# Ten or seven plain tiles in the first block, and who makes the low parts of the split ones

## The chip, the cores and the metric

The kernel runs on one core of a Trainium2 chip. The metric is the device time of one execution in microseconds (us); a kernel is run several times, and the median counts. The engines are TensorE (PE in the profile, PEld for its weight loads), VectorE (DVE), ScalarE (ACT), GpSimd (POOL) and SyncE (SP, which issues most DMAs). Each takes its instructions in a fixed order and waits for others through semaphores.

## The reference

Three parts run one after the other, all in float32; batch 4, 8 heads, 768 positions, so 3072 tokens of width 256:

```python
state = decay_full * state + sum(Bx, axis=2)          # a scan over chunks, per head
y     = (C @ B.T * L) @ x + (C @ state) * decay       # -> x, 3072 x 256
xn    = x / sqrt(mean(x * x) + 1e-6) * rms_g
g, v  = xn @ w_gate, xn @ w_val                       # 256 -> 1536 each
x     = (g * sigmoid(g) * v) @ w_out                  # 1536 -> 256
r     = maximum(x @ w_in, 0)                          # 256 -> 2048
out   = (s * r * r + b) @ w_out2                      # 2048 -> 256
```

The weights reach the chip as 64-bit floats and are turned into float32 there.

## The kernel before, in words

**Tiles and blocks.** The tokens come as 32 units of 96; seven blocks of 4 or 5 units (384 or 480 columns) go through the gated layer one after the other, then six groups of 512 columns through the second layer. The weights of the gated layer are cut into twelve tiles (F1 = 12) of 128 hidden features: a tile is 128x768 and holds two slices of w_gate, two of w_val and two of w_out. For a tile and a block, PE makes four hidden products (gate and value, two slices each), ACT takes Silu of the gate, DVE multiplies by the value, and PE makes two output products which add to the PSUM tiles o. The output products of a tile are put off until two more tiles have been emitted (LAG = 2).

**Two ways for a product.** A *split* tile uses the type float32r: a number is held as a high part (hi, a cast on ACT) and a low part (lo, number minus high part, on DVE), and `three` makes one product out of three: high times high, low times high, high times low. This needs the split of the weights (w1h, w1l; `split1`, line 745), of the tokens (xth, xtl) and of the activations (hi, lo in `hidden1`, line 799). A *plain* tile multiplies float32 by float32 (`hidden1_plain`, line 815), which the profile records as two records per product, and needs no split.

**The first block.** Blocks 1 to 6 use split tiles only. In block 0 the tiles 0 to 9 (PLAIN = 10) are plain and 10 and 11 are split. The first five plain tiles (HALVES) run in two halves of 192 columns, since the first units' tokens are ready before the others'. Each weight tile is decoded ahead of its use (`decode1`, line 737): five DVE passes over 768 elements (e, raw, w1f, e, w1f) and two on ACT (e, sg). A plain tile's weights stay in w1f until block 1 comes; there `split1` makes w1h and w1l of them (line 1091). The order of tiles in blocks 1 to 6 is ORDER: the split ones of block 0 first, then the plain ones.

**Token work.** Beside the tiles run the steps that make each unit's tokens: scan (DVE), gram products (PE) and m (DVE), y products (PE), squares (ACT), ss (DVE) and rs, a power of 128x2 elements (POOL), xn (ACT), transposes (PE), xth (ACT) and xtl (DVE). Units 4 to 7 are block 1's and are made while block 0 runs.

**The order.** All instructions are first collected in a plan (class `Plan`). `price` gives each a cost (for a POOL tensor_tensor over more than 128 elements n the cost is 3.1 ns x n + 0.06 us), `forward` and `backward` simulate the engines and due times, and `issue` emits the instructions in the order of the best of three passes. A change of any step may so reorder the others. Early gaps of PE are filled with products of ones. The plan has no cost for what an engine does to another that works at the same time, apart from a higher price of the small rs where `now_free` is off.

**Buffers.** Hidden products go to two PSUM buffers (tag h) in turn. The decoded tiles with m < PLAIN lie in the pool wlo, the others in the pool w2 with four buffers, which first hold first_bc and later x1 and raw tiles. The low parts w1l are in wlo as well.

The line numbers of the profile are those of the helper that emits the plan (L371) for nearly all instructions, so groups are told apart by the names of their tiles.

Of the kernel before, what the change touches and what calls it, by code (L numbers as in the profile page):

```python
# [40 lines left out]
LAG = 2  # L41
F1 = 12
F2 = 16
PLAIN = 10
HALVES = 5
ORDER = [*range(PLAIN, F1), *range(PLAIN)]
N2 = 512
# [338 lines left out]
def scan_glu_relu2(ctx: ExitStack, tc: tile.TileContext, bc, xr, aa, cst, w1, w2, gn, sv, bv, out):  # L386
    nc = Plan(tc.nc)
# [35 lines left out]
    w1h = {m: wts.tile([P, 6, P], F32R, tag="w1h", name="w1h") for m in ORDER}  # L423
    w1f, w1l, w2f, w2h = {}, {}, {}, {}
    w2_sum = const.tile([P, 2, P], F32, name="w2_sum")

    def f32(t):
        return t.bitcast(F32)
# [294 lines left out]
    def flat(t):  # L723
        return t.rearrange("p a b -> p (a b)")
# [12 lines left out]
    def decode1(m):  # L737
        if m not in raw1:
            load1(m)
        raw = raw1.pop(m)  # L740
        pool, tag = (wlo, "wlo") if m < PLAIN else (w2_p, "w2")
        w1f[m] = pool.tile([P, 6, P], F32, tag=tag, name="w1f")
        decode(raw, flat(w1f[m]), 6 * P, nc.vector)

    def split1(m):
        w1l[m] = wlo.tile([P, 6, P], F32R, tag="wlo", name="w1l")
        split(flat(w1f.pop(m)), flat(w1h[m]), flat(w1l[m]), nc.vector)


    def decode2(m):  # L750
# [17 lines left out]
    def split(src, hi, lo, rest=nc.vector):  # L768
        nc.scalar.copy(out=hi, in_=src)
        rest.tensor_tensor(out=lo, in0=src, in1=f32(hi), op=ALU.subtract)  # L770
# [44 lines left out]
    def hidden1_plain(j, m, half):  # L815
        n = NB[j] // 2
        cols = slice(0, NB[j]) if half is None else slice(half * n, (half + 1) * n)
        if half is None:
            ps = [ps_h.tile([P, 512], F32, tag="h", name="h")[:, :NB[j]] for v in range(2)]
        else:  # L820
            both = ps_h.tile([P, 512], F32, tag="h", name="h")
            ps = [both[:, v * n:(v + 1) * n] for v in range(2)]
        for v in range(2):
            for k in range(2):
                nc.pace = True
                nc.tensor.matmul(out=ps[v], lhsT=w1f[m][:, 2 * k + v, :],
                                 rhs=rows0[:, k, cols], start=k == 0, stop=k == 1)
                nc.pace = False
        s = hl_p.tile([P, cols.stop - cols.start], F32, tag="hi", name="h32")
        nc.scalar.activation(out=s, in_=ps[0], func=AF.Silu)  # L830
        nc.vector.tensor_tensor(out=s, in0=ps[1], in1=s, op=ALU.mult)

        def out():
            o = [t[:, :NB[j]] for t in o_t[j, 1]]
            for t in range(2):
                nc.pace = True
                nc.tensor.matmul(out=o[t][:, cols], lhsT=w1f[m][:, 4 + t, :], rhs=s,
                                 start=m == 0 and half == 0, stop=False)
                nc.pace = False
        pending.append(out)  # L840
# [151 lines left out]
    def drain(n):  # L992
        while len(pending) > n:
            pending.popleft()()
# [65 lines left out]
    for i in range(F1 + behind):  # L1060
        if i < F1:
            decode1(i)
            if i < HALVES:
                rows0 = xt_h[0]
                hidden1_plain(0, i, 0)
                drain(LAG)
            if i >= PLAIN:
                split1(i)
        tokens_to(count[1] + (count[3] - count[1]) * (i + 1) // behind if i < behind else
                  count[3] + (count[7] - count[3]) * (i + 1 - behind) // F1)  # L1070
        if i - behind == PLAIN:
            xt_h[0] = res_p.tile([P, 2, NB[0]], F32R, tag="res", name="xth0")
            xt_l[0] = [w2f_p.tile([P, NB[0]], F32R, tag="w2f", name="xtl0") for k in range(2)]
            for k in range(2):
                split(rows0[:, k], xt_h[0][:, k], xt_l[0][k])
        if i >= behind:
            if i - behind < PLAIN:
                hidden1_plain(0, i - behind, 1 if i - behind < HALVES else None)
            else:
                hidden1(0, i - behind)  # L1080
            drain(LAG)
# [7 lines left out]
    for i, (layer, j, m) in enumerate(plan):  # L1089
        at = i - start[layer, j]  # L1090
        if (layer, j) == (1, 1) and m < PLAIN:
            split1(m)
        if layer == 1 and 2 <= j < NBLK - 1 and at % 3 == 0:
            nc.floor = nc.latest
            decode2((j - 2) * 4 + at // 3)
            nc.floor = None
        late = at if layer == 1 and j == NBLK - 1 else F1 + m // 2 if (layer, j) == (2, 0) and m % 2 == 0 else None
        if late == 0:
            split_rows(0)
            bias_products()  # L1100
        for q in range(F2 // 2):
            if late == (max(2 * q, 1) if q < 7 else F1 + 2):
                combine(q)
        if layer == 2:
            if m == 0 and (g := j + 1) * N2 < 2 * NPAIR * SEQ:
                split_rows(g)
            if m % 2 == 0:
                seven(j, m // 2)
                drain(LAG)
            continue  # L1110
        hidden1(j, m)
        drain(LAG)
        for (i0, n0), (i1, n1) in zip(marks, marks[1:]):
            if i0 <= i < i1:
                tokens_to(n0 + -(-(n1 - n0) * (i + 1 - i0) // (i1 - i0)))
# [74 lines left out]
```

## Time and profile before

| | |
|---|---|
| median of 3 runs | 628.17 us (627.4 to 629.59) |
| span of the profiled execution | 626.8 us |
| PE busy | 617.4 us, 98% |
| DVE busy | 484.0 us, 77% |
| ACT busy | 447.5 us, 71% |
| POOL busy | 53.6 us, 9% |
| share of PE in the chain that ended last | 95% |
| granted TensorE clock, mean | 0.999 |

The span reaches from the first to the last instruction of one profiled execution; a run's time holds some 1.3 us more than that. Busy shares are means over stages of different kind, so the stages are read one by one below: up to about 30 us the weights and first tokens arrive, block 0 ends at about 74.5 us, block 1 follows, and so on. A row of a timeline gives start, duration, engine, line, operation, output and inputs, and count; neighbouring instructions of one kind are merged, and the duration is then that from the first start to the last end.

### The profile page before, as it was taken

How to read it: one execution, taken by the hardware profiler on the slowest of the kernel's cores; microseconds unless marked ns; L12 is line 12 of the kernel's file. 1: busy time of each engine (PE TensorE's matmuls, PEld its weight loads, DVE VectorE, ACT ScalarE, POOL GpSimd, SP SyncE). 2: the span in 40 equal slices, each digit the busy share in tenths (PEclk: the TensorE clock that was granted, in tenths of full speed). 3: DMA queues.
4: the chain of work that ended last, by engine and by line, in shares of the span. 5: the costliest groups of instructions: out<-in, count | busy, mean ns of one | idle time of the engine just before them, and what ended most of it. 6: DMA issues, size and time to landing. Idle time of an engine off the chain costs nothing.

```text
span 626.8 us, 12902 instructions
## 1 busy us (share of the span) xinstructions
PE 617.4 (98%) x4937; PEld 546.9 (87%) x4937; DVE 484.0 (77%) x972; ACT 447.5 (71%) x941; POOL 53.6 (9%) x88
## 2 busy tenths in 40 slices
PE   9999999999999999999999999999999999999996
PEld 8786899999988888888888889999999999999986
DVE  7999965778756765766865568798897897987975
ACT  5797553766645545664664579898898999988985
POOL 3001100010100001102232220000000000000000
PEclk9999999999999999999999999999999999999999
DMA  6966413424404423400100000001010010010101
GB/s 219 245 216 186 130 29 67 89 70 102 112 34 89 104 81 86 105 20 2 27 2 1 0 2 0 2 5 31 1 34 1 2 35 0 9 28 1 33 1 36
DMA packets 33695, 35.01 MB, mean 56 GB/s; under 512 B 14048, under 2 KB 30048, under 8 KB 33632
## 3 DMA queue, kind: packets, MB, share of 16 engines
q1 hardware_dynamic: 32688, 33.71, 20.9%
q8 instruction: 39, 0.64, 0.4%
q10 hardware_dynamic: 944, 0.46, 0.3%
q14 instruction: 24, 0.20, 0.1%
HBM read 30.90 MB, written 3.25 MB: 54 GB/s over the span
## 4 chain that ended last, share of the span: by engine, by line
PE 95%; ACT 2%; DMA 1%; DVE 1%; issue 0%; DVEq 0%; ACTq 0%
PE h L371 54%; PE o L371 22%; PE acc L371 13%; PE y L371 5%; DMA raw<-in_w 1%; PE o L364 1%; ACT sg L371 0%; ACT xh L371 0%; DVE res L371 0%; ACT xn L371 0%; ACT e L371 0%; PE ab L371 0%; DVE m L371 0%; ACT xth L371 0%; DVE a_sb L371 0%
## 5 line engine op out<-in xcount | busy, mean ns | idle before, releaser
L371 ACT ACTIVATE s<-h 128x512 f32<-128x512 f32 (+2 forms) x170 | 97.3, 572 | 44.0 <-PE h L371 40.7
L371 ACT CAST hi<-s 128x256 fp32r<-128x256 f32 (+2 forms) x170 | 80.1, 474 | 64.4 <-DVE s L371 62.3
L371 PE MATMUL h<-x1h,w2h 128*128 128x512 f32 x384 | 119.2, 391 | 0.0
L371 DVE TENSOR_TENSOR lo<-s,hi 128x256 fp32r<-128x256 f32 (+2 forms) x170 | 86.9, 512 | 30.8 <-ACT hi L371 28.3
L371 PE MATMUL h<-xth,w1h 128*128 128x480 f32 (+1 forms) x296 | 109.9, 371 | 0.5 <-DVE s L371 0.5
L371 PE MATMUL h<-xth,w1l 128*128 128x480 f32 (+1 forms) x296 | 109.0, 368 | 0.0
L371 PE MATMUL h<-xtl,w1h 128*128 128x480 f32 (+1 forms) x296 | 107.8, 367 | 0.0
L371 PE MATMUL acc<-hi,w2c 128*128 128x256 f32 x448 | 81.7, 281 | 0.0
L371 PEld LDWEIGHTS h<-x1h,w2h 128*128 128x128 f32 x384 | 69.2, 188 | 12.3
L371 DVE TENSOR_TENSOR s<-h,s 128x480 f32<-128x480 f32 (+1 forms) x74 | 45.8, 619 | 41.7 <-PE h L371 36.1
L371 PE MATMUL h<-x1l,w2h 128*128 128x512 f32 x192 | 75.0, 390 | 0.0
L371 PEld LDWEIGHTS acc<-hi,w2c 128*128 128x128 f32 x448 | 71.0, 189 | 2.3
L371 DVE TENSOR_TENSOR added<-s 128x256 f32<-128x256 f32 x144 | 56.6, 421 | 13.4 <-ACT s L371 12.4
L371 PE MATMUL acc<-lo,w2c 128*128 128x256 f32 x224 | 63.2, 282 | 0.0
L371 PEld LDWEIGHTS h<-xth,w1h 128*128 128x128 f32 x296 | 55.5, 188 | 7.7 <-DVE s L371 1.0
L371 ACT ACTIVATE s<-s 128x512 f32<-128x512 f32 x96 | 60.2, 633 | 1.9
L371 PEld LDWEIGHTS h<-xth,w1l 128*128 128x128 f32 x296 | 55.6, 188 | 6.1 <-issue 0.2
L371 PEld LDWEIGHTS h<-xtl,w1h 128*128 128x128 f32 x296 | 55.6, 188 | 5.6 <-issue 0.2
L371 PE MATMUL o<-hi,w1l 128*128 128x480 f32 (+1 forms) x148 | 54.2, 367 | 0.0
L371 PE MATMUL o<-hi,w1h 128*128 128x480 f32 (+1 forms) x148 | 54.1, 366 | 0.0
L371 PE MATMUL o<-lo,w1h 128*128 128x480 f32 (+1 forms) x148 | 53.9, 365 | 0.0
L371 DVE TENSOR_TENSOR lo<-added,hi 128x768 fp32r<-128x768 f32 x48 | 45.9, 957 | 0.5 <-ACT hi L371 0.5
(98 smaller groups left out, 1071.0 us busy)
## 6 DMA issues: line engine op xcount, KB each, us to landing
raw<-in_w SPq DMA_DIRECT2D x12, 768.0 KB, 5.4
raw<-in_w SPq DMA_DIRECT2D x16, 512.0 KB, 3.7
a_sb<-a_scr SPq DMA_DIRECT2D x28, 196.0 KB, 3.9
xh<-in_xr SPq DMA_DIRECT2D x60, 48.0 KB, 1.9
raw_bc<-in_bc SPq DMA_DIRECT2D x56, 32.0 KB, 3.8
raw_bc<-in_bc SPq DMA_DIRECT2D x112, 16.0 KB, 1.7
out_t<-res SPq DMA_DIRECT2D x13, 96.0 KB, 1.9
out_t<-res SPq DMA_DIRECT2D x5, 144.0 KB, 1.9
```

Source lines behind the costliest of these rows:

```text
L364: self.nc.tensor.matmul(out=idle, lhsT=ones, rhs=ones, start=not fills, stop=True, skip_group_check=True)
L371: getattr(engine, op["fn"])(*op["args"], **op["kw"])
```

## The change

Two lines. PLAIN goes from 10 to 7, so tiles 7, 8 and 9 run as split tiles in block 0 and ORDER becomes 7 to 11, then 0 to 6. And `split1` takes GpSimd for the low part of the tiles from PLAIN on (7 to 11, in block 0), DVE still for the others (0 to 6, in block 1).

```diff
-PLAIN = 10
+PLAIN = 7
 HALVES = 5
 ORDER = [*range(PLAIN, F1), *range(PLAIN)]
...
     def split1(m):
         w1l[m] = wlo.tile([P, 6, P], F32R, tag="wlo", name="w1l")
-        split(flat(w1f.pop(m)), flat(w1h[m]), flat(w1l[m]), nc.vector)
+        split(flat(w1f.pop(m)), flat(w1h[m]), flat(w1l[m]), nc.vector if m < PLAIN else nc.gpsimd)
```

The function that it calls is unchanged; `rest` is the engine of the low part:

```python
def split(src, hi, lo, rest=nc.vector):
    nc.scalar.copy(out=hi, in_=src)
    rest.tensor_tensor(out=lo, in0=src, in1=f32(hi), op=ALU.subtract)
```

## Rows read from the trace of the kernel before

**Rows 1.** The table of stretches: busy time (x instructions) of each engine, clock, DMA.
```profile
core 0: us, PE busy (x) PEld busy (x) DVE busy (x) ACT busy (x) POOL busy (x), PEclk, DMA share, GB/s
30.00:62.00 32.00, 31.43 (x257) 24.14 (x263) 31.84 (x61) 27.48 (x55) 2.69 (x1) 1.00 0.66 205
62.00:87.00 25.00, 25.00 (x244) 21.76 (x227) 24.63 (x44) 12.29 (x32) 2.19 (x1) 1.00 0.35 97
87.00:112.00 25.00, 25.00 (x314) 23.79 (x313) 11.73 (x25) 11.97 (x34) 0.69 (x1) 1.00 0.34 64
```
**Rows 2.** The chain that ended last, 30 to 90 us: start, us, what.
```profile
43.76 2.58 PE h L371 x8
...
54.88 1.29 PE o L371 x4
...
80.05 2.12 PE h L371 x12
82.17 1.05 PE o L371 x6
```
**Rows 3.** The timeline of DVE at the end of block 0.
```profile
61.45 0.95 DVE L371 TENSOR_TENSOR w1f<-w1f,e 128x768 f32<-128x768 f32 x1
...
62.78 1.41 DVE L371 TENSOR_TENSOR m<-y,a_sb 128x384 f32<-128x384 f32 x4
64.11 0.95 DVE L371 TENSOR_TENSOR w1l<-w1f,w1h 128x768 fp32r<-128x768 f32 x1
...
66.77 0.95 DVE L371 TENSOR_TENSOR w1l<-w1f,w1h 128x768 fp32r<-128x768 f32 x1
...
67.71 0.95 DVE L371 TENSOR_TENSOR w1f<-w1f,e 128x768 f32<-128x768 f32 x1
68.58 0.95 DVE L371 TENSOR_TENSOR w1l<-w1f,w1h 128x768 fp32r<-128x768 f32 x1
...
69.92 0.95 DVE L371 TENSOR_TENSOR w1l<-w1f,w1h 128x768 fp32r<-128x768 f32 x1
...
71.66 0.54 DVE L371 TENSOR_TENSOR lo<-s,hi 128x384 fp32r<-128x384 f32 x1
```
**Rows 4.** The timeline of ACT: the casts of tiles 10 and 11.
```profile
62.43 0.84 ACT L371 CAST w1h<-w1f 128x768 fp32r<-128x768 f32 x1
...
68.70 0.83 ACT L371 CAST w1h<-w1f 128x768 fp32r<-128x768 f32 x1
```
**Rows 5.** Groups by line and shape, 0 to 70 us: busy, mean ns | idle before.
```profile
L371 ACT CAST w1h<-w1f 128x768 fp32r<-128x768 f32 x12 | 9.8, 856 | 0.1
```
**Rows 6.** The timeline of POOL; in brackets the idle time before and its releaser.
```profile
67.89 2.19 POOL L371 TENSOR_TENSOR rs<-ss,fixed 128x2 f32<-128x2 f32 x1 [11.69 <-DVE ss L371]
...
157.57 0.74 POOL L371 TENSOR_TENSOR w_sum<-w_sum,w2f 128x256 f32<-128x256 f32 x1 [10.66 <-DVE w2f L371]
...
295.97 0.47 POOL L371 TENSOR_TENSOR sums<-w2f 128x128 f32<-128x128 f32 x1
...
303.08 1.50 POOL L371 TENSOR_TENSOR sums<-w2f 128x256 f32<-128x256 f32 x1
...
315.88 0.79 POOL L371 TENSOR_TENSOR w_sum<-w_sum,w2f 128x256 f32<-128x256 f32 x1
```
**Rows 7.** The timeline of DVE beside the POOL operation of 303.08.
```profile
303.96 0.77 DVE L371 TENSOR_TENSOR w2c<-w2f,w2c 128x128 fp32r<-128x128 f32 x1
```
**Rows 8.** The tile w2c, 314 to 318 us: duration ns min/median/max, first and last start.
```profile
L371 DVE TENSOR_TENSOR w2c<-w2f,w2c x6: 280/286/823, 314.2 to 316.7; 128x128 fp32r<-128x128 f32 x6
```
**Rows 9.** Groups of DVE by shape, 46 to 69 us: those that read PSUM.
```profile
L371 DVE TENSOR_TENSOR h<-h,h 128x384 f32<-128x384 f32 x5 | 2.8, 553 | 0.0
...
L371 DVE TENSOR_TENSOR m<-y,a_sb 128x384 f32<-128x384 f32 x4 | 2.0, 550 | 0.0
...
L371 DVE SCALAR_TENSOR_TENSOR xtl<-y,sb,xth 128x96 fp32r<-128x96 f32 x4 | 1.0, 312 | 0.0
L371 DVE TENSOR_TENSOR m<-y,a_sb 128x128 f32<-128x128 f32 x4 | 1.0, 282 | 0.0
```
**Rows 10.** The timeline of PE where block 1 begins.
```profile
74.53 0.34 PE L371 MATMUL h<-xth,w1h 128*128 128x384 f32 x1
```

## The prediction

> **What bounds the kernel now.** I read the table of stretches first. From 30 us on TensorE (PE) is busy almost without a gap, and up to 87 us VectorE (DVE) is too: 31.84 of 32 us, then 24.63 of 25. Only after 87 us does DVE fall to 11.73 of 25 [rows 1]. So the first block, which ends near 74.5 us, has two engines that are full at once. After it PE alone sets the time, and whatever the first block loses or gains goes unchanged to the end. Then I read the chain of waits for PE's price of a tile, the timelines of DVE and ScalarE (ACT) for the end of the block, and the rows where GpSimd (POOL) works beside DVE. The profiled span is 626.8 us and the median of the runs 628.17, so 1.3 us lie around the span; I work out the difference on the span and add it to the median.
>
> **PE.** The eight records of a plain tile's four hidden products take 2.58 us in the chain, its four output records 1.29, together 3.87 us. A split tile's twelve hidden products take 2.12 us, its six output products 1.05, together 3.17 us [rows 2]. Three tiles change sides: 3 x 0.70 = 2.1 us less PE work, all ahead of block 1. That is the most the change can give.
>
> **DVE, what leaves.** The subtraction that makes a low part is a 128x768 DVE pass: 0.95 us recorded, 0.87 from start to start. Tile 10's decode ends at 61.45 + 0.95 = 62.40, ACT casts it at 62.43, so its low part is the pass at 64.11. Tile 11's decode ends at 67.71 + 0.95 = 68.66, its cast starts at 68.70, so its low part is that at 69.92. The passes at 66.77 and 68.58 belong to tiles that block 1 needs [rows 3, 4]. The change gives the low parts of tiles 10 and 11 to POOL, and the one at 66.77 is no longer urgent, since block 1 starts with five tiles already split. Ahead of the end of tile 11's decode DVE so loses 2 x 0.87 = 1.74 us (64.11 and 66.77).
>
> **DVE, what comes.** A split tile also needs the low part of its own activations, a 128x384 subtraction of 0.54 us (71.66), about 0.46 in a dense row [rows 3]. Tiles 7, 8 and 9 add 3 x 0.46 = 1.4 us. ACT adds three casts of about the same size. Between 62 and 87 us it is busy 12.29 of 25 us [rows 1], and all twelve weight casts already lie before 70 us [rows 5], so ACT's part costs nothing; without that cover it would be half a microsecond a cast.
>
> **DVE, what GpSimd does to it.** The trace has no 128x768 POOL subtraction. Its nearest rows are 128x128 in 0.47 us and 128x256 in 0.74: 2.1 ns an element more, so 0.74 + 512 x 2.1 ns = 1.8 us for 768 elements, an estimate from these two [rows 6]. That is twice DVE's time, but POOL is nearly idle. What matters is DVE beside it. At 303.96 a w2c subtraction takes 0.77 us, while a POOL addition of 128x256 runs to 303.08 + 1.50 = 304.58 [rows 6, 7]; six such subtractions near 315 us take 0.28 us at the least, 0.29 in the middle and 0.82 at the worst, and that one stands beside the POOL addition of 315.88 [rows 6, 8]. The two lose 0.49 and 0.54 us against 0.28, or 1.9 to 2.1 ns for each of the 256 elements: DVE stands still for nearly as long as POOL runs. For 768 elements this makes 1.6 us a tile, more than the 0.87 that DVE is spared.
>
> [...]
>
> The other end is zero. A two-element rs operation on POOL at 67.89 takes 2.19 us, while the DVE pass inside it (68.58) keeps its 0.95 us: there POOL did the waiting [rows 3, 6]. And DVE passes that read PSUM need not be stopped: m, h and xtl from y take 2.0 + 1.0 + 2.8 + 1.0 = 6.8 of the 23 us from 46 to 69 us [rows 9]. What of a POOL operation falls beside them would cost DVE nothing. So the loss of a tile lies between 0 and 1.6 us. Three tenths off give 1.1; and as the m passes at 62.78 stand where tile 10's low part becomes ready [rows 3], I take 1.0. Four tiles (7 to 10) fall ahead of the end of tile 11's decode: 4.0 us, with ends 0 and 6.4.
>
> **The end of block 0.** PE takes its instructions in order. Tile 11's second product needs the low part, and behind it stand the rest of tile 11 and all of block 1, which begins at 74.53 today [rows 10]. In the changed kernel:
> - tile 11's decode ends later by 4.0 + 1.4 - 1.74 = 3.7 us;
> - from the cast's end (68.70 + 0.83 = 69.53 [rows 4]) to the end of the DVE low part (69.92 + 0.95 = 70.87) it is 1.34 us; POOL takes 1.8 and perhaps half a microsecond until a DVE pass lets it in, 2.3: 1.0 us more;
> - the six output products of tile 10, 1.05 us, which stand ahead of block 1 today, can fill PE's wait: 1.05 us back;
> - the order of instructions is planned, and tile 11's decode may go ahead of token work such as the m passes at 62.78. But block 1 waits for that work as well, and both are in one full engine. I give this 1.0 us, with bounds 0 and 2.
>
> Sum: 3.7 + 1.0 - 1.05 - 1.0 = 2.6 us later for block 1. The 2.1 us that PE saves become idle PE time.
>
> **Cost at nothing.** POOL's own queue: rs of the units of block 1 now stands among five operations of about 2 us each, and ACT's scaling, PE's transposes and the xth tiles wait for rs; where rs lands right behind a low part it is up to 2 us late, which the upper end holds. Block 1: DVE has seven low parts left after 74.5 us instead of eight, but PE is busy all the time there [rows 1], so nothing is gained. DMAs: none is moved, and the weights load in the order 0 to 11 as before. Buffers: the decoded tiles 7 to 9 move to another pool, where tile 11 takes the buffer of tile 7; that low part is done some 15 us before. Below nothing: the planner's new order of later instructions could win a few tenths, but PE has no gap there to win.
>
> **Rivals.**
> - *The full gain.* POOL waits, as rs did, and DVE isn't stopped. With no loss the sum is 2.6 - 4.0 = -1.4 us, and with the planner's slack at its bound of 2 us PE's own saving is reached: 628.2 - 2.1 = 626.1 us. For it: the rs row. Against it: the w2c rows, subtractions on both engines as here. It decides below about 0.1 us lost a tile.
> - *A wash.* At 0.4 us a tile the sum is 2.6 - 4.0 + 1.6 = 0.2 us: 628.4. It holds from 0.2 to 0.8 us a tile, 627.6 to 630.0. For it: the PSUM passes, and that the low parts of tiles 7 and 8 come while decoding is still ahead of PE. Against it: most of what DVE has to do reads SBUF twice.
> - *All of it lost.* Each of the four tiles costs 1.6 us and the planner's microsecond goes to a late rs: 6.4 + 1.4 - 1.74 + 1.0 - 1.05 = 6.0 us: 634.2.
> - *Another order only.* The split tiles run so late that they lie among block 1's, DVE's loss is hidden there and PE's saving shows in part: 627 us. Against it: two hidden PSUM buffers hand the tiles over in turn.
>
> **How the numbers follow.** Chances: the forecast 0.47, all of it lost 0.08, the wash 0.31, the full gain 0.11, another order 0.03. The predicted time is 628.2 + 2.6 = 630.8 us, and the forecast's own range 629.6 to 632.5. A difference of 0.3%, 1.9 us, is about what a measurement of this kernel can tell from no change: below 626.3 is faster, above 630.1 slower. Slower: 0.42 of the forecast and all of it lost, 0.50. Faster: the full gain and a little of the last case, 0.13. The rest, 0.37, is the same. The 8-in-10 range runs from just under the full gain, 626.0, to 633.5, short of all of it lost.
>
> **What would show it.** In the changed profile: five POOL subtractions w1l of 1.8 us or more; DVE passes with two SBUF inputs stretched beside them, from 0.95 to 2 us or more; PE waiting for a POOL w1l at tile 11 and perhaps at tiles 9 and 10; block 1's first product at 76 to 78 us against 74.53. The step on DVE is wrong if its passes keep their durations beside POOL; the sum is wrong if block 1 starts before 74 us; and the first block's seven plain tiles must show 2.1 us less PE work, or the change does not do what it says.

## The result and the profile after

The changed kernel takes 634.92 us (median of 4 runs, 634.26 to 636.18) against 628.25 for the kernel before in the same session (4 runs): the ratio is 1.0102, 95% interval 1.0085 to 1.0119, so it is slower by 6.7 us. The forecast was 630.8 us, 2.6 more than before, with a range that ended at 633.5. The profiled execution is the slowest of the four (636.18, span 634.4), so its rows sum to a little more than the median shows. Its time holds 1.8 us more than its span, not 1.3; differences between runs don't feel that.

First the timeline of PE, where block 2 begins. Block 1's first product is a poor marker here, since different output products are still pending when it starts; at block 2 they are all done. The first fence is the kernel before, the second the changed one (start us, us, engine, line, operation, tiles). The row at 71.29 is the second product of tile 11 in the kernel before, the one that needs its low part; it is used further down.

```profile
71.29 0.33 PE L371 MATMUL h<-xth,w1l 128*128 128x384 f32 x1
...
119.56 0.34 PE L371 MATMUL h<-xth,w1h 128*128 128x384 f32 x1
```
```profile
126.40 0.34 PE L371 MATMUL h<-xth,w1h 128*128 128x384 f32 x1
```

Block 2 is 6.84 us late. Nearly all of the loss is there, and nothing after it gives any back: from here to the last instruction the profiled executions differ by another 0.8 us (spans of 634.4 and 626.8).

The table of stretches, which answers to [rows 1], with one more stretch:

```profile
30.00:62.00 32.00, 28.04 (x227) 22.71 (x225) 31.81 (x56) 25.37 (x53) 10.03 (x4) 0.99 0.64 202
62.00:87.00 25.00, 23.44 (x201) 21.81 (x202) 24.13 (x38) 13.23 (x32) 5.63 (x4) 0.88 0.34 99
...
62.00:68.00 6.00, 6.00 (x47) 5.34 (x48) 5.84 (x10) 2.70 (x5) 2.27 (x2) 0.50 0.11 30
```

DVE is as full as before (31.81 of 32 us) and now PE isn't: it is busy for 28.04 us where it was 31.43. In 62 to 68 us its granted clock is 0.50. Next the timelines of POOL, DVE, ACT and PE around the end of block 0, which answer to [rows 3], [rows 4], [rows 6] and [rows 10]:

```profile
52.05 5.08 POOL L371 TENSOR_TENSOR w1l<-w1f,w1h 128x768 fp32r<-128x768 f32 x2
60.62 1.82 POOL L371 TENSOR_TENSOR w1l<-w1f,w1h 128x768 fp32r<-128x768 f32 x1 [3.49 <-ACT w1h L371]
65.06 1.83 POOL L371 TENSOR_TENSOR w1l<-w1f,w1h 128x768 fp32r<-128x768 f32 x1 [2.62 <-ACT w1h L371]
...
73.27 2.10 POOL L371 TENSOR_TENSOR w1l<-w1f,w1h 128x768 fp32r<-128x768 f32 x1 [1.02 <-ACT w1h L371]
...
52.98 2.46 DVE L371 SCALAR_TENSOR_TENSOR w1f<-raw 128x768 f32<-128x768 uint32 x1
55.36 2.19 DVE L371 TENSOR_SCALAR e<-raw 128x768 uint16<-128x768 uint16 x1
...
61.51 1.76 DVE L371 TENSOR_TENSOR_SCAN a_sb<-a_sb,delta 128x392 f32<-128x392 f32 x1
...
64.92 1.39 DVE L371 TENSOR_TENSOR m<-y,a_sb 128x384 f32<-128x384 f32 x4
66.23 1.08 DVE L371 TENSOR_SCALAR e<-raw 128x768 uint16<-128x768 uint16 x1
...
68.88 0.95 DVE L371 SCALAR_TENSOR_TENSOR w1f<-raw 128x768 f32<-128x768 uint32 x1
...
70.21 0.55 DVE L371 TENSOR_TENSOR lo<-s,hi 128x384 fp32r<-128x384 f32 x1
...
70.75 0.95 DVE L371 TENSOR_TENSOR w1f<-w1f,e 128x768 f32<-128x768 f32 x1
...
72.77 3.44 DVE L371 TENSOR_TENSOR_SCAN a_sb<-a_sb,delta 128x392 f32<-128x392 f32 x2 [0.33 <-DMA a_sb<-a_scr]
76.12 0.53 DVE L371 TENSOR_TENSOR s<-h,s 128x384 f32<-128x384 f32 x1
...
77.91 0.55 DVE L371 TENSOR_TENSOR lo<-s,hi 128x384 fp32r<-128x384 f32 x1
...
72.37 0.83 ACT L371 CAST w1h<-w1f 128x768 fp32r<-128x768 f32 x1
...
54.67 0.44 PE L371 MATMUL h<-xth,w1l 128*128 128x384 f32 x1 [1.09 <-POOL w1l L371]
...
59.87 0.44 PE L371 MATMUL h<-xth,w1h 128*128 128x384 f32 x1 [2.10 <-ACT s L371]
...
76.70 0.45 PE L371 MATMUL h<-xth,w1h 128*128 128x384 f32 x1 [1.52 <-DVE s L371]
...
78.14 0.34 PE L371 MATMUL h<-xth,w1l 128*128 128x384 f32 x1
```

Read each POOL row against the DVE rows inside it. The pass w1f<-raw that takes 0.95 us alone (68.88) takes 2.46 at 52.98, the pass e that takes 0.55 alone takes 2.19 at 55.36: 1.51 and 1.64 us lost to the first two subtractions. The third costs a scan 0.79 (1.76 against 0.97), the fourth a pass e 0.53, the fifth the second of the two scans at 72.77 1.60 (the pair takes 3.44, and 1.84 in the run nolock below). That is 6.07 us in all, 4.47 of it ahead of the end of tile 11's decode. The four m passes at 64.92, which read PSUM, keep their duration beside the fourth subtraction (1.39 us, and 1.41 at 62.78 in the kernel before); only the pass behind them is stopped.

The chain of waits of the changed kernel (start, us, what) says what these stops are worth:

```profile
53.00 2.43 DVE w1f L371
55.43 2.13 DVE e L371
...
57.58 0.94 ACT e L371
58.52 0.92 ACT xth L371 x4
59.44 0.39 ACT s L371
...
68.15 4.52 DMA a_sb<-a_scr
...
72.77 1.60 DVE a_sb L371 x2
74.37 1.76 issue
76.12 0.54 DVE s L371
```

Two stopped DVE passes delay e on ACT, which stands ahead of the Silu that PE wants: this is PE's wait of 2.10 us at 59.87. Later the two scans of units 8 and 9 wait for their DMA until 72.77; the fifth stop stands in the chain as 1.76 us of "issue", time in which the profile shows nothing that DVE waited for. Behind it comes s of tile 10 (76.12), for which PE waits. POOL's own result, the low part of tile 11, was ready at 75.37.

### The profile page after: what moved, and what is told of

It reads as the page before. It is cut to its first block, busy times and chain, and to the rows that moved or that the text cites. A ratio compares the mean times of both kernels' runs of the same rounds, so it can differ in the third digit from the quotient of the medians.

```text
span 634.4 us, 12937 instructions
## 1 busy us (share of the span) xinstructions
PE 620.3 (98%) x4943; PEld 551.6 (87%) x4943; DVE 486.8 (77%) x970; ACT 448.4 (71%) x944; POOL 64.3 (10%) x93
## 4 chain that ended last, share of the span: by engine, by line
PE 87%; DVE 5%; ACT 4%; DMA 2%; issue 2%; DVEq 0%; SPq 0%; ACTq 0%
PE h L371 48%; PE o L371 19%; PE acc L371 13%; PE y L371 5%; DMA a_sb<-a_scr 2%; PE o L364 1%; ACT sg L371 1%; DVE w1f L371 1%; DVE s L371 1%; DVE e L371 1%; PE ab L371 1%; ACT e L371 1%; DVE a_sb L371 1%; ACT xth L371 1%; DVE m L371 0%
## 5 line engine op out<-in xcount | busy, mean ns | idle before, releaser
L371 PE MATMUL h<-xth,w1h 128*128 128x480 f32 (+1 forms) x308 | 114.3, 372 | 5.0 <-ACT s L371 2.7
L371 PE MATMUL h<-xth,w1l 128*128 128x480 f32 (+1 forms) x308 | 113.8, 370 | 1.1 <-POOL w1l L371 1.1
L371 PE MATMUL h<-xtl,w1h 128*128 128x480 f32 (+1 forms) x308 | 112.6, 369 | 0.0
L371 DVE TENSOR_TENSOR s<-h,s 128x480 f32<-128x480 f32 (+1 forms) x77 | 47.4, 615 | 42.3 <-PE h L371 36.3
L371 PEld LDWEIGHTS h<-xth,w1h 128*128 128x128 f32 x308 | 58.3, 189 | 13.5 <-ACT s L371 4.0
L371 PEld LDWEIGHTS h<-xth,w1l 128*128 128x128 f32 x308 | 58.3, 189 | 7.8 <-POOL w1l L371 1.7
L371 PEld LDWEIGHTS h<-xtl,w1h 128*128 128x128 f32 x308 | 58.4, 190 | 5.6 <-issue 0.2
L371 PE MATMUL o<-hi,w1h 128*128 128x480 f32 (+1 forms) x154 | 56.5, 367 | 0.0
L371 PE MATMUL o<-hi,w1l 128*128 128x480 f32 (+1 forms) x154 | 56.5, 367 | 0.0
L371 PE MATMUL o<-lo,w1h 128*128 128x480 f32 (+1 forms) x154 | 55.8, 365 | 0.0
```

Source lines behind the costliest of these rows:

```text
L371: getattr(engine, op["fn"])(*op["args"], **op["kw"])
```

## The experiments

Three theories were open. POOL's subtractions stop DVE, and the stops carry the loss. Or three more split tiles cost time by themselves, whoever makes the low parts. Or PE's clock, which fell between 62 and 68 us, carries it. The runs take these one at a time. All times are medians of runs beside the kernel before on the same chip (628.4 to 628.5 us).

**idlepool: the stop alone.** The kernel before, and POOL does five subtractions of 128x768 that nobody reads and nobody waits for:

```diff
+            w = op["kw"].get("out")
+            if op["eng"] == "vector" and op["fn"] == "tensor_tensor" and w.name.startswith("w1f"):
+                self.made += 1
+                if self.made > F1 - 5:
+                    self.nc.gpsimd.tensor_tensor(out=self.spare, in0=w, in1=w, op=ALU.subtract)
```

> The kernel before, every instruction of DVE, ACT, PE and SP in its order, and five GpSimd subtractions 128x768 (w1f minus itself, into a tile that nobody reads), each ready when one of the tiles 7 to 11 is decoded. Nobody waits for their result. Theory A: DVE stops for about 1.2 us beside each; since DVE is full this comes through but for its slack of some 2 us: 631 to 634 us. Rival B (only the wait for the low part matters): 627.5 to 629 us.

631.89 us, ratio 1.0056 (1.0041 to 1.0071): 3.4 us slower, inside the first theory's range. The first of the five, on POOL and beside it on DVE, and an ACT row at the end of the block, in the timelines:

```profile
44.68 2.18 POOL L377 TENSOR_TENSOR spare<-w1f 128x768 bf16<-128x768 f32 x1 [16.77 <-DVE w1f L372]
...
45.95 1.73 DVE L372 SCALAR_TENSOR_TENSOR w1f<-raw 128x768 f32<-128x768 uint32 x1
...
73.62 0.84 ACT L372 ACTIVATE xn<-y,rs 128x256 f32<-128x256 f32 x2 [2.09 <-POOL rs L372]
```

The order of every other engine is that of the kernel before, and nobody waits for these results, yet four DVE passes are 3.5 us longer in sum (0.78 for the one shown, 1.73 against 0.95; then 1.09, 0.80 and 0.81). The fourth subtraction, at 63.89, stands beside m passes that read PSUM (four in 1.41 us at 64.13) and stops nothing. From the first stop to the end of tile 11's decode DVE loses 2.4 us for 2.67 us of stops: tile 7's last decode pass starts at 43.64 us where it was 44.66 before, tile 11's decode ends at 70.02 where it was 68.66. So there a microsecond of stopped DVE is nearly a microsecond of the block. The whole 3.4 us can't be put on the stops alone, though: rs stands behind the fifth subtraction in POOL's queue, ACT waits 2.09 us for it, and DVE then 0.98 us for the hi behind that.

**nolock: the change without the reading.** POOL writes the low parts (one column copied, then two fills with zeros: 1.77 us for the third tile, from 58.94 on, where a lone subtraction takes 1.82) but doesn't read the tiles; the low parts of the five tiles are zero. The order is that of the changed kernel.

```diff
+                engine.tensor_copy(out=lo[:, 0:1], in_=hi[:, 0:1])
+                for _ in range(2):
+                    engine.memset(lo.bitcast(F32), 0.0)
```

> The changed kernel in the same order on every engine, but GpSimd only writes: each of its five 128x768 subtractions is a copy of one column of w1h (which keeps the wait for the cast) and two memsets of w1l; the low parts are zero, so that part of the weights is left out. Theory A (GpSimd's reading stops the DVE passes that read SBUF twice; the changed profile has them 6.1 us longer in all): the passes keep 0.95 and 0.55 us, block 1 starts 5 to 6 us earlier than in the changed kernel, time 627 to 630 us. Rival B (GpSimd's time from cast to low part, and its queue, make PE wait): GpSimd still takes about 1.5 us a tile, so little changes: 632 to 635 us. Rival C (three more split tiles are simply too much for the first block, whoever makes the low parts): 634 to 635 us.

631.99 us, ratio 1.0053 (1.0036 to 1.0069): 2.9 us less than the changed kernel, still 3.5 us more than the kernel before. That is 2 us above the first theory's range and at the lower edge of that of rival B, whose wait shows only at tile 7 (1.04 us, for POOL's w1l at 54.81). POOL, DVE and PE in the timelines of this run, and two stretches of its table:

```profile
53.22 1.53 POOL L375 MEMSET w1l<- 128x768 f32 x2
...
53.16 0.96 DVE L377 SCALAR_TENSOR_TENSOR w1f<-raw 128x768 f32<-128x768 uint32 x1
54.03 1.13 DVE L377 TENSOR_SCALAR e<-raw 128x768 uint16<-128x768 uint16 x1
...
66.95 0.94 DVE L377 TENSOR_TENSOR w1f<-w1f,e 128x768 f32<-128x768 f32 x1
...
70.38 1.84 DVE L377 TENSOR_TENSOR_SCAN a_sb<-a_sb,delta 128x392 f32<-128x392 f32 x2 [2.02 <-DMA a_sb<-a_scr]
...
72.72 0.44 PE L377 MATMUL h<-xth,w1h 128*128 128x384 f32 x1 [1.83 <-DVE s L377]
```
```profile
68.00:73.00 5.00, 3.17 (x18) 2.84 (x17) 2.98 (x5) 2.82 (x7) 2.10 (x4) 1.00 0.64 130
73.00:77.00 4.00, 4.00 (x17) 3.99 (x16) 4.00 (x9) 1.42 (x6) 0.00 (x0) 0.57 0.92 359
```

The stops are gone but for 0.58 us (54.03), and tile 11's decode ends at 67.89, 3.81 us before the changed kernel's 71.70 (70.75 + 0.95). That is the 4.47 - 0.58 = 3.89 us of stops, nearly one for one. At that point nolock is 0.8 us ahead of the kernel before, and yet it ends 3.5 us behind it: DVE stands 2.02 us before the scans, PE 1.83 us for the s behind them, and then PE runs at a granted 0.57.

**double: twice the stops.** Each of POOL's five subtractions is issued twice.

```diff
-            getattr(engine, op["fn"])(*op["args"], **op["kw"])
+            for _ in range(1 + (op["eng"] == "gpsimd" and "out" in op["kw"] and op["kw"]["out"].name.startswith("w1l"))):
+                getattr(engine, op["fn"])(*op["args"], **op["kw"])
```

> The changed kernel with each of the five GpSimd subtractions done twice (the same result), every order unchanged. Theory A: DVE stops for up to 1.6 us more beside each, and PE waits 1.8 us more for each low part: 639 to 643 us, with the DVE passes stretched by 10 to 13 us in all against 6.1. Rival C: the low parts are only a little late: 635 to 637 us.

642.26 us, ratio 1.0215 (1.0198 to 1.0232), inside the first theory's range: 7.3 us more than the changed kernel for five more subtractions, 1.5 each. The timelines of POOL and DVE:

```profile
52.24 13.83 POOL L372 TENSOR_TENSOR w1l<-w1f,w1h 128x768 fp32r<-128x768 f32 x6
...
53.16 2.46 DVE L372 SCALAR_TENSOR_TENSOR w1f<-raw 128x768 f32<-128x768 uint32 x1
55.55 2.15 DVE L372 TENSOR_SCALAR e<-raw 128x768 uint16<-128x768 uint16 x1
```

Here the two engines take turns, one instruction each: six DVE passes in a row, from 53.16 on, are 1.5 to 1.65 us longer, one beside each of the six subtractions, and these take 2.3 us each (13.83 in all), where a lone one takes 1.82. In sum DVE's passes are 14.0 us longer (10 to 13 were expected, 6.07 in the changed kernel), and PE also waits 3.6 us for a low part, so the 7.3 us aren't stops alone. The first theory holds, but for a part of the loss only: idlepool and nolock put the subtractions at about 3 us of the 6.7.

**vec7, vec8, vec9: fewer plain tiles, DVE makes all low parts.** `split1` is that of the kernel before; only PLAIN differs.

```diff
-PLAIN = 10
+PLAIN = 7        # 8 and 9 in the other two
```

> One part alone: seven plain tiles, all low parts on DVE. Theory A: DVE gets 1.4 us for activations and 1.7 us of low parts more ahead of tile 11 than in the kernel before, no stalls: 629 to 631.5 us, clearly below the changed kernel's 634.9. Rival C: 634 to 635.5 us, the same as the changed kernel.

> Eight plain tiles, all low parts on DVE. At 1.2 us a tile: 630.5 to 631.2 us. With slack for one tile only: 629 to 630 us.

> Nine plain tiles, all low parts on DVE. If every tile turned from plain to split costs DVE about 1.2 us in a full first block (three cost 3.7 us): 629.4 to 630 us. If DVE has slack for one (1.7 us of low parts that block 1 needs stand early in the kernel before) and TensorE's 0.7 us come through: 627.5 to 628.2 us.

vec7 632.19 (1.0053, 1.0037 to 1.0069), vec8 630.35 (1.0027, 1.0018 to 1.0037), vec9 628.08 (1.0006, 0.9988 to 1.0023). The 3.7 us of vec7 are above what was expected of it; vec8 lies between its two ranges; vec9 falls in the second of its ranges, that in which DVE has slack for one tile. So the second theory has something in it too: each split tile in the place of a plain one saves PE time on paper, and none makes the kernel faster; one makes no difference, two cost 1.9 us with the granted clock at 1.00 to 87 us, three 3.7 us without any work on POOL. Of these 3.7 most are the clock's, as vec7_awake shows below.

**pool10: only the engine changed.** PLAIN stays 10; POOL makes the low parts of tiles 10 and 11 alone.

```diff
-        split(flat(w1f.pop(m)), flat(w1h[m]), flat(w1l[m]), nc.vector)
+        split(flat(w1f.pop(m)), flat(w1h[m]), flat(w1l[m]), nc.vector if m < PLAIN else nc.gpsimd)
```

> The other part alone: ten plain tiles as before, the low parts of tiles 10 and 11 on GpSimd. Theory A: two GpSimd subtractions stop DVE for 1.2 us each against 1.74 us taken off it, and tile 11's low part comes 1 us later: 628.5 to 630.5 us. Rival C: DVE is relieved, nothing else changes: 627 to 628.3 us.

631.31 us, ratio 1.0047 (1.0034 to 1.0060): 2.9 us for two subtractions, above the expectation. DVE in its timeline:

```profile
62.04 2.10 DVE L371 TENSOR_SCALAR raw<-raw 128x768 int32<-128x768 int32 x1
...
68.06 4.29 DVE L371 TENSOR_TENSOR w1l<-w1f,w1h 128x768 fp32r<-128x768 f32 x3
```

Both stops are whole (1.55 us at 62.04; 1.6 in the row of three, which take 2.7 alone), 3.15 together, while DVE was spared two low parts, 1.74 us. Tile 11's decode ends 1.0 us earlier than in the kernel before (67.66 against 68.66): the loss comes behind it, where the second stop stands ahead of s of tile 10 and PE waits 1.61 us for that s (at 72.94). The two halves of the change, 3.7 (vec7) and 2.9, add to 6.6 of the 6.7 us, but that is chance: 2.7 of vec7's 3.7 are a fall of the clock (next runs), which costs the changed kernel nothing that can be measured.

**vec7_awake, awake, awake2: the clock.** Products of ones that nobody reads keep PE busy where it waited: 44 of them in vec7, ahead of tile 10's first product; 92 in the changed kernel at tiles 7 and 8 (awake); the same and 38 ahead of tile 11's second half (awake2).

```diff
+            for _ in range(self.extra.get(i, 0)):
+                self.nc.tensor.matmul(out=idle, lhsT=ones, rhs=ones, start=False, stop=True, skip_group_check=True)
...
+                nc.extra[len(nc.ops)] = {(7, 1): 40, (8, 0): 40, (8, 1): 12, (11, 1): 38}.get((m, v), 0)
```

> Seven plain tiles with all low parts on DVE, and 44 products of ones put on TensorE ahead of tile 10's first product, where it stalled for 2.5 us in that kernel before it ran at a granted clock of 0.5 from 64.9 to 71.6 us. Theory D (here the clock lies on the path, since DVE then waited 1.4 and 0.9 us for products): the clock stays 1.0 and 1.5 to 2.5 us come back: 629.7 to 630.7 us against 632.2. Rival (DVE alone sets the time, as where the same was tried with GpSimd): 631.7 to 632.7 us.

> The changed kernel with 92 products of ones put on TensorE where it stalled (40 and 12 ahead of tile 8's two halves, 40 ahead of the second half of tile 7), the other engines' order unchanged. Theory D (the granted clock of 0.5 from 61.7 to 68.2 us lies on the path): clock stays 1.0 and 2 to 3 us come back: 632 to 633 us. Theory A (DVE is the bound there, TensorE waits anyway): the clock stays 1.0 and the time stays at 634 to 635.5 us.

> The changed kernel with TensorE kept busy by products of ones that nobody reads: the 92 of the run awake at tiles 7 and 8, and 38 more ahead of tile 11's second half, where awake's granted clock fell to 0.50 (77 to 80 us) once PE had waited 2.1 us for the DVE pass that makes s of tile 10. Nothing else differs, in order or work. If the clock lies on the path that delays the output half of tile 11 and with it block 1: 632.5 to 634 us, with the granted clock at 1.0 up to 85 us and block 2's first product ahead of the 126.4 us that both the changed kernel and awake show. Rival, the DVE queue alone sets that end and PE would have waited for it at either clock: 634 to 635.5 us, block 2's first product at 126 us or later, clock at 1.0 all the same.

vec7_awake 629.53 (1.0012, 1.0001 to 1.0023), just under the range of the theory that the clock counts; awake 635.39 (1.0108, 1.0093 to 1.0123) and awake2 634.76 (1.0100, 1.0085 to 1.0116), both in the range in which it doesn't. The tables of stretches of vec7, vec7_awake, awake and awake2:

```profile
60.00:65.00 5.00, 2.26 (x11) 1.56 (x10) 5.00 (x10) 2.37 (x4) 0.00 (x0) 0.99 0.18 53
65.00:71.00 6.00, 6.00 (x77) 5.67 (x77) 4.62 (x9) 2.88 (x9) 0.69 (x1) 0.50 0.60 113
```
```profile
60.00:65.00 5.00, 4.78 (x79) 4.34 (x80) 5.00 (x11) 2.91 (x4) 0.00 (x0) 1.00 0.14 39
65.00:71.00 6.00, 6.00 (x81) 5.67 (x74) 6.00 (x12) 5.21 (x15) 0.69 (x1) 1.00 0.59 114
```
```profile
77.00:80.00 3.00, 3.00 (x11) 3.00 (x11) 3.00 (x8) 0.74 (x4) 0.00 (x0) 0.50 0.52 202
```
```profile
62.00:68.00 6.00, 6.00 (x127) 5.30 (x127) 6.00 (x10) 3.82 (x6) 2.15 (x2) 1.00 0.12 33
77.00:80.00 3.00, 2.96 (x18) 2.61 (x17) 3.00 (x8) 1.52 (x5) 0.00 (x0) 1.00 0.79 309
```

In vec7 the clock counts. PE had been busy for 2.26 of 5 us, waiting for a cast, and then ran at 0.50; DVE was busy only 4.62 of the next 6 us, since it waited for PE. With the fills both go, and 2.7 us with them; 1.0 us over the kernel before is left. In the changed kernel the clock counts for nothing that can be measured. awake didn't settle that, since its clock fell later instead (77 to 80 us). In awake2 it is at 1.00 in every stretch from 50 to 87 us, PE still waits for s of tile 10 (38 fills and 0.42 us), block 2 begins at 126.06 (126.40 in the changed kernel), and the time is that of the changed kernel. There DVE is last, and a faster PE waits longer.

**late, nolock_late: the scans.** The scans of units 8 and 9 are held back until s of tile 11 has been made, in the changed kernel and in nolock.

```diff
+        after = start[self.release] + 1e-6
+        start = [max(t, after) if i in self.held else t for i, t in enumerate(start)]
...
+            if units[0] == 8:
+                nc.held.add(len(nc.ops))
...
+        if (j, m) == (0, F1 - 1):
+            nc.release = len(nc.ops)
```

> The changed kernel with one thing moved: the two scans of units 8 and 9 (block 2's), which stood on DVE ahead of the activation product s of tile 10 and waited there for their DMA (started at 72.77, done at 76.2 us), come behind the s of tile 11. All other instructions keep their order. Theory E (the place of these scans is a cause of its own): PE's wait of 1.5 us for s goes, 632.5 to 633.7 us against 634.9. Rival (the fifth GpSimd subtraction, done at 75.4 us, ends last anyway, or stops another pass): 634.2 to 635.2 us.

> Both undone: GpSimd only writes (low parts zero, so that part of the weights is left out) and the two scans come late. Theories A and E add up: 2 to 3 us under the 632.0 us of the kernel in which GpSimd only writes, since DVE waited 2.0 us for the DMA there: 629 to 630.2 us, near the kernel before. Rival C (seven plain tiles are too much for DVE): 631 to 632.5 us, no better than with the scans early.

late 634.09 (1.0115, 1.0078 to 1.0151; its six runs spread from 633.69 to 640.28), nolock_late 630.54 (1.0036, 1.0019 to 1.0052). Each lies between its two ranges, late just under the rival's. DVE in the timeline of late:

```profile
72.90 0.56 DVE L374 TENSOR_TENSOR s<-h,s 128x384 f32<-128x384 f32 x1 [0.78 <-PE h L374]
73.38 1.49 DVE L374 TENSOR_TENSOR lo<-s,hi 128x384 fp32r<-128x384 f32 x1
```

With the scans out of the way s of tile 10 starts 3.2 us earlier (72.90 for 76.12), but the fifth subtraction then stops the low part behind it (1.49 for 0.55). The difference to the changed kernel, 0.8 us, can't be told from none. Without stops the same edit gains 1.45 us; since the granted clock then stays at 1.00, where nolock's fell to 0.57, scans and clock can't be told apart in that. The edit has a price of its own, too: in block 1 PE waits 0.76 us (late, at 82.90) and 0.75 us (nolock_late, at 78.88) for an s that now stands behind the scans. Between these two runs, alike in order and both without a fall of the clock, lies the cleanest price of the stops: 634.09 - 630.54 = 3.55 us. nolock_late still stands 2.1 us above the kernel before. PE idles 1.9 of 12 us between 50 and 62 us in it, for POOL's w1l and for s on ACT, nearly what the three tiles save it. How the 2.1 divide further wasn't tried, and what they consist of is not shown.

## Why the prediction was wrong

**PE: right.** The records of full-width plain hidden products in block 0 go from 40 to 16, three tiles' worth. PE's saving did become idle time, as the text had it: 4.0 us idle in 30 to 62 us, 0.6 before. The saving itself was read from the number of records, not measured as 2.1 us.

**What GpSimd does to DVE: right, at the right size.** A lone subtraction takes 1.82 us, as estimated. Four stops ahead of the end of tile 11's decode cost 4.47 us, where 4.0 were taken (1.1 a tile for 1.0). PSUM passes were spared, as supposed (the m passes at 64.92). The two-input pass at 52.98 is stopped for 1.51 us beside a subtraction; in nolock the two-input pass at 53.16 keeps 0.96 us beside a fill. The prediction read 1.6 us a tile from the w2c rows; where a stop isn't covered by other passes it measures 1.51 to 1.64.

**The end of tile 11's decode: right in the sum, by luck in two terms.** Predicted 3.7 later, less 1.0 for the planner: 2.7. Measured 71.70 against 68.66, 3.04 later. Put the measured stops in the place of the 4.0 and the sum is 4.47 + 1.4 - 1.74 - 1.0 = 3.1. nolock tests the same sum without stops: 0.58 + 1.4 - 1.74 - 1.0 = -0.8 us, and its decode ends 0.77 us early. But the planner's 1.0 us isn't what it was said to be. Just as many passes of token work stand ahead of the decode's end as before (8 scans, 16 m passes, 4 xtl from y). What stands behind it instead is work of the split tiles: two low parts of activations came ahead of it and not three (the second is the one at 70.21), and one product with the value fewer, together about 0.9 us.

**The rest of "The end of block 0": wrong.** This is the step that failed. From 2.7 late at the decode the prediction went to 2.6 late at block 1; the trace goes from 3.04 to 6.84 late at block 2. Three things make the difference.
- The low part of tile 11 was priced 1.0 us longer and is 1.46 longer (71.70 to 75.37, 3.67 us, against 2.21 before). The cast starts 0.67 us after the decode, since s and a copy stand before it on ACT. From the cast's end (72.37 + 0.83 = 73.20) to the end of the subtraction it is 2.17 us, near the 2.3 that were taken; the subtraction takes 2.10, and whether the 0.28 above a lone one is a wait for a DVE pass is not shown.
- Tile 11 then didn't wait for that low part. Its second product ran at 78.14, 2.77 us after it, where it was 0.42 before (71.29 against 69.92 + 0.95 = 70.87): 2.35 us which the sum doesn't have. In 1.33 of the 2.77 us PE stood still; in the rest it worked off what its order has behind that wait. PE's queue stood at s of tile 10, and s stood on DVE behind the scans and the fifth stop. The prediction counted four stops, because the fifth comes after tile 11's decode. DVE had three tiles' s and lo still to do then (9, 10 and 11; two tiles', 10 and 11, in the kernel before), and was as critical after the decode as before it.
- The 1.05 us of tile 10's output products were to fill PE's wait and came behind it, the first at 77.78. They need s and lo of tile 10, and lo was made at 77.91, on the engine that caused the wait.

In sum 3.04 + 1.46 + 2.35 = 6.85 us. Against the prediction's 2.65 that is 0.34 in the decode, 0.46 in the low part, 2.35 between that low part and its use, where PE waits for DVE's queue, and 1.05 of credit.

Seen through the runs the same error reads otherwise. With stops taken as nothing the prediction's sum was 2.6 - 4.0 = -1.4 us. nolock_late, which has only 0.6 us of stops, came out at +2.1; vec7_awake, which has none but leaves the low parts on DVE, at +1.0. The stops themselves were worth 2.9 to 3.6 us (nolock, and late against nolock_late), not more than predicted. What was mis-sized is the rest: three more split tiles were taken to be slightly good for the end of the block, and in both runs they are bad for it.

**What would show it.** The five POOL subtractions and the DVE passes of over 2 us are there. PE did wait for a POOL w1l, but at tile 7 (1.09 us at 54.67) and not at tile 11. Block 1's first product came at 80.36, outside the 76 to 78.

**The rivals.** *All of it lost* came nearest in time (634.2), but not by its mechanism: the stops didn't cost 1.6 us for each of four tiles, and no rs was late in the chain. *The full gain* needed POOL to wait for DVE; the trace shows DVE waiting (2.46 us for 0.95 at 52.98). *A wash* rested on PSUM passes beside the subtractions. That happened at the third and fourth, which cost 0.79 and 0.53 us, and it wasn't enough. *Another order only* didn't happen: the split tiles stand ahead of block 1's first product.

## What to carry to other kernels

Where two engines are full in the same stretch, moving work from one to a third engine helps only if the third leaves the others' time alone; here each 128x768 subtraction on GpSimd spared DVE 0.87 us and took up to 1.6. Follow the sum to the last consumer: a credit such as "other products fill the wait" holds only if their inputs don't come from the engine that makes the wait. And count what a full engine still has to do behind the last instruction that you priced, since a stop there can cost as much: the fifth took 1.60 us of DVE, right ahead of the s for which PE waited 1.52.

## What the runs showed of the hardware

- One-input DVE passes were stopped as well as two-input ones: TENSOR_SCALAR on integers goes from 0.55 to 2.19 us beside a POOL subtraction (55.36 in the changed kernel). In nolock one takes 1.13 while POOL fills and then copies a column (54.03), another keeps 0.54 beside fills (63.05), and the two-input pass at 53.16 keeps 0.96.
- TensorE's granted clock fell from 1.00 to 0.50 in the changed kernel, after 8.24 busy us of 12 with a longest wait of 2.10 us, and in vec7, after 2.26 of 5 with one of 2.51; in nolock it fell to a mean of 0.57, after 3.17 of 5 with one of 1.83. It didn't fall each time: late was busy for 8.23 us of the same 12, with a longest wait of 2.1, and its clock in 62 to 68 us was 1.00.
- Such a fall cost 2.7 us in vec7 (632.19 against 629.53 us) and nothing that can be measured in the changed kernel, where DVE was last (634.92 against 634.76 in awake2).
